# Respreading casts, evacuations and relus over ScalarE and VectorE, with smaller weight staging and deeper pools, in a fused window-attention and channel-mix kernel

## The chip, the cores and the metric

The kernel runs on one core of a Trainium2 chip. The metric is the device time of one execution in microseconds (us), as the median of several runs. TensorE is called PE here, VectorE DVE, ScalarE ACT and GpSimd POOL; SP is SyncE, whose queue issues nearly all transfers.

## The reference

Two stages follow each other. First comes attention over a sliding window of 128 positions plus 4 sink positions; then a channel mix works on the attention's output.

```python
# q, k, v: (4, 8, 768, 64) f32; n_sink = 4, window = 128
scores = (q @ k.T) / sqrt(64), kept where pos < 4 or 0 <= i - j < 128
a = softmax(scores);  x = a @ v, as (4, 768, 512)
# channel mix; w_k: (512, 1024), w_v: (1024, 512), w_r: (512, 512)
xk = mu_k * x + (1 - mu_k) * x_prev      # x_prev: x one position earlier
xr = mu_r * x + (1 - mu_r) * x_prev
k = relu(xk @ w_k);  v = (k * k) @ w_v;  r = sigmoid(xr @ w_r)
return r * v                             # (4, 768, 512) f32
```

## The kernel before

The work is cut into 12 units of 256 positions: batch b has tiles T = 0, 1, 2, and unit u = 3 b + T. The stages of a unit and the tiles that they fill are these.

- **prepare**: q, k and v (f32) land in `qs`, `ks`, `vs`, three buffers each. Half tiles of q and k are cast to bf16 into `qb` and `kb` (lines 526 and 529), transposed by PE into a PSUM bank (L550) and evacuated into `qt` and `kt` (L560). For k from unit 4 on and q from unit 8 on, a DMA transposes instead (L537, issued by SP). v is cast into `vb` (L575), which has a column of ones for the softmax sums. In the first unit of a batch POOL copies the sink keys (`ksink`), and PE and DVE make the sink values (`vsink`).
- **attend**: sink scores (L611) with an exponential into `es`; scores of two head pairs at a time (L635) into `sc`; ACT's exponential into `e` (L657); DVE's mask (L671); the product with `vb` (L682, L694); DVE's reciprocal (L707) and scaling into `x` (L710).
- **mix**: PE transposes `x` (L733), the result is evacuated into `xt` (L744), and DVE makes the difference `td` (L758) and eight pieces of `xk` and `xr` (L768).
- **ffn**: eight blocks of keys with `wk_sb` (L818), relu into `rl` (L827), DVE's square into `kk` (L831), two gates with `wr_sb` (L841), tanh into `th` (L847), four blocks of products with `wv_h` (L859), DVE's final product into `ob` (L868), and a store. The last unit's last product is cut in two (L788, L798).

The f32 weights are loaded in five transfers of 1 MB: `wka`, `wkb` (column halves of w_k), `wr`, `wva`, `wvb` (row halves of w_v). Each of the three matrices has f32 staging of its own, and DVE casts them in ten pieces to bf16 (L501, L503).

PSUM holds two double-bank tiles `sc` and four single banks (`bank`), which the transposes, keys, gates, values and products share.

No scheduler runs at execution time. A list `ORDER` gives for each of PE, DVE, ACT, POOL and SP the numbers of its operations in order, and every engine runs its list strictly in that order. The class `Plan` walks the lists with assumed costs to decide two things: which buffer of a pool each operation takes, and where PE's list gets filler matmuls (L879) on a tile `warm`, which keep PE's clock up while there is no work. Which engine does an operation is fixed in the source: for unit 0 DVE casts q, k and v and evacuates q; all other casts of q and k and all other evacuations are ACT's; POOL casts v from unit 1 on, and DVE casts all weights.

Of the kernel before, what the change touches and what calls it, by code (L numbers as in the profile page):

```python
# [17 lines left out]
CAST = {"k": "ACT", "q": "ACT"}  # L18

CAST0 = {"k": "DVE", "q": "DVE"}  # L20
EVAC0 = {"k": "ACT", "q": "DVE", "x": "ACT"}
# [14 lines left out]
LOADS = ("kq0", "v0", "kq1", "wka", "v1", "wkb", "wr", "wva", "wvb")  # L36
WCAST = ("DVE",) * 10
VCAST = ("DVE", "POOL")
# [6 lines left out]
        92, 89, 98, 105, 95, 116, 108, 113, 128, 141, 124, 119, 131, 137, 103, 148, 134, 157,  # L45
        155, 168, 219, 211, 207, 212, 220, 208, 160, 176, 165, 171, 183, 189, 215, 193, 200,
        223, 180, 216, 225, 237, 298, 186, 290, 302, 291, 303, 299, 294, 248, 295, 227, 235,
        231, 263, 232, 228, 260, 306, 266, 318, 240, 256, 245, 251, 310, 276, 269, 311, 283,
        326, 329, 308, 321, 314, 343, 315, 370, 378, 352, 366, 371, 379, 332, 367, 374, 382,
        337, 375, 384, 359, 348, 386, 396, 387, 421, 390, 274, 444, 391, 452, 445, 453, 426,  # L50
        407, 448, 456, 394, 449, 457, 460, 399, 464, 404, 465, 415, 462, 410, 430, 472, 499,
        578, 437, 468, 474, 504, 469, 525, 583, 526, 537, 485, 538, 533, 509, 529, 534, 530,
        477, 553, 482, 488, 493, 545, 511, 564, 518, 549, 541, 546, 543, 550, 601, 609, 605,
        602, 556, 610, 606, 567, 631, 613, 561, 572, 614, 617, 587, 619, 621, 594, 629, 622,
        634, 625, 639, 626, 642, 677, 689, 678, 681, 663, 690, 682, 645, 707, 685, 650, 686,
        695, 701, 670, 718, 705, 702, 693, 697, 710, 698, 760, 715, 761, 756, 768, 757, 769,
        721, 726, 764, 742, 765, 772, 749, 740, 784, 780, 774, 781, 795, 834, 830, 835, 842,
        831, 787, 843, 838, 792, 798, 860, 776, 803, 816, 839, 777, 823, 846, 848, 854, 858,
        855, 871, 910, 918, 906, 911, 907, 850, 863, 851, 919, 868, 936, 874, 914, 879, 915,
        930, 892, 924, 899, 931, 926, 947, 934, 922, 944, 939, 927, 976, 972, 977, 984, 973,  # L60
        985, 950, 980, 955, 958, 981, 988, 990, 965, 992, 996, 993, 997, 1012, 1000, 1013, 1004,
        1001, 1005, 1008, 1016, 1009, 1020, 1018, 1021, 1028, 1024, 1029, 1025,
    ),
    "DVE": (
        70, 91, 88, 93, 97, 71, 94, 99, 100, 107, 112, 101, 123, 109, 114, 110, 118, 115, 120,
        125, 143, 121, 126, 146, 144, 78, 145, 150, 79, 151, 152, 81, 164, 154, 104, 159, 147,
        175, 170, 161, 80, 162, 177, 166, 178, 167, 172, 153, 173, 82, 83, 202, 195, 196, 210,
        69, 197, 203, 204, 198, 206, 84, 85, 205, 199, 214, 218, 239, 293, 301, 222, 86, 305,
        87, 255, 297, 250, 233, 244, 229, 241, 242, 257, 246, 247, 252, 258, 253, 325, 320, 278,
        312, 279, 285, 280, 287, 322, 286, 327, 323, 328, 331, 316, 281, 289, 288, 282, 354,  # L70
        333, 334, 336, 369, 373, 338, 355, 339, 377, 361, 381, 362, 356, 363, 388, 275, 357,
        392, 364, 365, 398, 358, 403, 447, 451, 414, 455, 400, 459, 401, 409, 405, 406, 466,
        416, 417, 411, 412, 432, 433, 434, 439, 441, 440, 435, 470, 442, 481, 476, 528, 436,
        510, 487, 492, 478, 532, 479, 483, 443, 489, 484, 494, 490, 495, 540, 555, 560, 513,
        536, 514, 520, 516, 515, 522, 521, 547, 551, 523, 571, 517, 566, 557, 558, 604, 524,
        568, 569, 562, 563, 573, 574, 608, 633, 612, 616, 589, 592, 590, 638, 623, 635, 591,
        596, 598, 597, 627, 636, 640, 641, 593, 599, 644, 600, 665, 649, 646, 680, 692, 647,
        684, 651, 652, 714, 666, 688, 709, 672, 667, 674, 703, 668, 675, 673, 711, 725, 699,
        712, 676, 716, 720, 669, 717, 722, 723, 727, 759, 728, 763, 744, 767, 745, 751, 771,
        746, 753, 752, 741, 786, 782, 747, 755, 791, 797, 788, 789, 833, 793, 799, 802, 794,  # L80
        800, 748, 804, 845, 805, 754, 837, 778, 841, 825, 818, 821, 819, 820, 826, 829, 827,
        867, 856, 862, 822, 878, 909, 864, 873, 865, 852, 913, 869, 870, 875, 876, 880, 828,
        881, 917, 921, 894, 943, 897, 932, 895, 938, 896, 901, 905, 902, 945, 903, 940, 941,
        928, 949, 946, 954, 904, 951, 952, 898, 956, 975, 957, 960, 979, 961, 963, 987, 962,
        983, 967, 969, 970, 968, 971, 994, 964, 998, 1003, 1007, 1015, 1011, 1022, 1030, 1026,
    ),
    "ACT": (
        67, 68, 90, 111, 106, 96, 122, 117, 127, 130, 136, 142, 129, 132, 133, 149, 138, 163,
        135, 158, 156, 169, 174, 221, 213, 182, 209, 188, 184, 190, 201, 194, 179, 185, 224,
        181, 217, 226, 238, 187, 243, 292, 262, 300, 304, 296, 254, 249, 236, 264, 259, 265,  # L90
        261, 307, 267, 319, 268, 324, 277, 270, 284, 342, 340, 309, 330, 335, 344, 345, 347,
        353, 372, 380, 368, 420, 425, 383, 376, 360, 498, 418, 349, 385, 397, 422, 503, 423,
        402, 496, 454, 427, 446, 413, 450, 395, 458, 408, 461, 501, 577, 582, 575, 463, 431,
        473, 500, 438, 579, 475, 480, 505, 584, 527, 486, 491, 535, 531, 539, 559, 554, 512,
        519, 565, 580, 542, 544, 653, 570, 655, 603, 611, 607, 657, 632, 615, 618, 588, 659,
        637, 630, 620, 731, 595, 735, 643, 648, 679, 664, 691, 683, 729, 713, 708, 687, 671,
        696, 733, 808, 724, 706, 694, 719, 806, 762, 810, 758, 770, 743, 766, 812, 750, 785,
        790, 775, 773, 801, 882, 796, 836, 832, 844, 866, 861, 840, 817, 824, 849, 847, 884,
        859, 888, 886, 872, 877, 912, 908, 942, 920, 916, 893, 937, 925, 900, 935, 948, 923,
        953, 978, 974, 986, 959, 989, 982, 991, 966, 1014, 1002, 1006, 1010, 1019, 1017,  # L100
    ),
    "POOL": (
        77, 72, 73, 75, 76, 74, 102, 139, 140, 191, 192, 271, 273, 272, 350, 351, 428, 506, 429,
        585, 507, 661, 508, 586, 662, 737, 738, 739, 814, 815, 890, 891,
    ),
    "SP": (
        1, 3, 0, 2, 4, 5, 6, 7, 8, 11, 9, 10, 16, 12, 15, 13, 20, 14, 19, 17, 18, 21, 22, 25,
        23, 234, 24, 30, 341, 28, 35, 346, 313, 29, 317, 26, 33, 27, 389, 38, 34, 40, 31, 419,
        424, 36, 393, 497, 230, 32, 502, 37, 41, 43, 576, 39, 467, 44, 45, 581, 46, 47, 656, 42,
        548, 51, 654, 471, 52, 660, 658, 49, 552, 628, 57, 50, 48, 55, 56, 53, 730, 732, 736,  # L110
        58, 734, 54, 704, 61, 807, 811, 809, 813, 63, 700, 783, 64, 624, 62, 883, 59, 60, 885,
        889, 887, 857, 65, 853, 779, 66, 929, 933, 999, 995, 1023, 1031, 1027,
# [4 lines left out]
class Plan:  # L117
# [17 lines left out]
    def op(self, engine, cost, emit, rank, reads=(), writes=(), take=(), hold=(), port=False,  # L135
           lag=None, service=0.0, descs=128, mode=0):
        self.ops.append(dict(engine=engine, cost=cost, emit=emit, rank=rank, reads=list(reads),
                             writes=list(writes), take=list(take), hold=list(hold), port=port,
                             lag=90.0 if lag is None else lag, service=service, descs=descs, mode=mode))

    def schedule(self):
# [42 lines left out]
        while any(lines.values()):  # L184
# [35 lines left out]
            if o["service"]:  # L220

                descs = o["descs"]
# [9 lines left out]
                flying.append((dma, descs))  # L232
# [39 lines left out]
def kernel(  # L272
# [36 lines left out]
    for name in ("ks", "qs", "vs"):  # L309
        pool(name, 3, [128, 2, H, D] if name == "vs" else [128, H, 2, D], FP32)  # L310
    pool("kb", 3, [128, 2, H, D], BF16)
    pool("qb", 3, [128, 2, H, D], BF16)
    pool("kt", 4, [128, NP, 2, 128], BF16)
    pool("qt", 3, [128, NP, 2, 128], BF16)
# [5 lines left out]
    pool("xk", 3, [128, NC, 256], BF16)  # L320
    pool("xr", 3, [128, NC, 256], BF16)
    pool("kk", 2, [128, NF, 256], BF16)
    pool("rl", 4, [128, 2, 256], BF16)
    pool("th", 4, [128, Dm], FP32)
    pool("ob", 3, [128, Dm], FP32)
    pool("vb", 3, [128, 2, H, D + 1], BF16)
    buf = P.buf

    def tile1(shape, dtype, name):
        return const.tile(shape, dtype, name=name)  # L330


    def dve(n, rate=1.04):
        return 64.0 + rate * n

    def act(n):
        return 67.0 + 0.833 * n
# [593 lines left out]
```

## Time and profile before

| what | value |
|---|---|
| median of 5 runs (lowest to highest) | 172.39 us (172.27 to 172.66) |
| the profiled execution's own time | 172.39 us |
| its span, first to last instruction | 170.7 us |
| PE busy, matmuls | 163.0 us, 1624 |
| DVE busy, instructions | 148.5 us, 372 |
| ACT busy, instructions | 132.4 us, 219 |
| POOL busy, instructions | 26.9 us, 47 |
| DMA packets, bytes | 82803, 33.82 MB |
| filler matmuls (L879) | 44, 13.1 us |
| granted PE clock | 1.00 throughout |

The profiled execution's time equals the median of the runs; 1.7 us of it lie outside the span. Durations in the profile are those of single instructions. On DVE and ACT one instruction starts before the one ahead of it has ended, so the spacing of starts in a dense stretch is shorter than a duration. Matmuls overlap still more: a row's mean is a latency, and the spacing says what a matmul costs.

### The profile page before, as it was taken

The numbers are of one execution on the slowest core, as the hardware profiler recorded it, in microseconds if no ns is written. First come the engines' busy times: TensorE is split into PE (matmuls) and PEld (weight loads), VectorE is DVE, ScalarE is ACT, GpSimd is POOL, SyncE is SP. The second block draws the span as 40 slices with busy tenths as digits, with TensorE's granted clock in tenths as the row PEclk, the third lists the DMA queues.
The fourth block names the chain that finished last, engine by engine and source line by source line (L and its number), as shares of the span: only waits on it lengthen the run. The fifth ranks groups of instructions, "written<-read, shape, count | busy, mean of one in ns | idle before, by whom it ended". The sixth has DMA issues, their size and how long they took to land.

```text
span 170.7 us, 4235 instructions
## 1 busy us (share of the span) xinstructions
PE 163.0 (96%) x1624; PEld 107.9 (63%) x1624; DVE 148.5 (87%) x372; ACT 132.4 (78%) x219; POOL 26.9 (16%) x47
## 2 busy tenths in 40 slices
PE   7898988999999999999999999999999999999992
PEld 2345576575758567667658568577585775684751
DVE  2497998999899778899999999998999999999632
ACT  3169987999999999999879979977887938654330
POOL 6130080005400020124301200120300203000000
PEclk9999999999999999999999999999999999999999
DMA  4999999998968999999757998976989985030203
GB/s 103 234 272 376 287 284 359 352 257 188 297 171 212 224 254 254 162 231 208 187 131 142 256 226 222 227 147 175 174 232 180 185 205 139 0 127 0 108 15 123
DMA packets 82803, 33.82 MB, mean 198 GB/s; under 512 B 64736, under 2 KB 77280, under 8 KB 82784
## 3 DMA queue, kind: packets, MB, share of 16 engines
q1 hardware_dynamic: 81728, 33.56, 84.6%
q8 instruction: 12, 0.20, 0.5%
q10 hardware_dynamic: 1056, 0.00, 0.3%
q14 instruction: 7, 0.06, 0.1%
HBM read 24.12 MB, written 6.29 MB: 178 GB/s over the span
## 4 chain that ended last, share of the span: by engine, by line
PE 81%; DMA 6%; SPq 6%; POOL 2%; ACT 1%; DVE 1%; issue 1%
PE bank L818 24%; PE bank L859 24%; PE bank L841 12%; DMA vs<-in_v_dram 6%; PE sc L635 6%; PE bank L694 6%; PE bank L733 3%; SPq L377 3%; SPq L360 2%; PE bank L550 2%; PE bank L682 2%; PE bank L611 2%; POOL vb L575 2%; SPq L397 1%; PE bank L788 1%
## 5 line engine op out<-in xcount | busy, mean ns | idle before, releaser
L818 PE MATMUL bank<-xk,wk_sb 128*128 128x256 bf16 x384 | 48.9, 273 | 0.0
L657 ACT ACTIVATE e<-sc 128x1024 bf16<-128x1024 f32 (+1 forms) x48 | 45.0, 976 | 4.9 <-PE sc L635 4.9
L859 PE MATMUL bank<-wv_h,kk 128*128 128x512 bf16 x184 | 46.4, 379 | 0.0
L818 PEld LDWEIGHTS <-wk_sb 128*128 128x128 bf16 x384 | 35.6, 98 | 7.1 <-issue 0.2
L575 POOL CAST vb<-vs 128x512 bf16<-128x512 f32 x22 | 20.0, 918 | 109.8 <-DMA vs<-in_v_dram 83.0
L827 ACT ACTIVATE rl<-bank 128x512 bf16<-128x512 f32 x48 | 27.6, 609 | 9.1 <-PE bank L818 8.5
L671 DVE TENSOR_TENSOR e<-e,mask 128x1024 bf16<-128x1024 bf16 (+1 forms) x48 | 30.7, 649 | 0.4 <-ACT e L657 0.4
L859 PEld LDWEIGHTS <-kk 128*128 128x128 bf16 x184 | 16.7, 98 | 14.7 <-DVE kk L831 0.3
L841 PE MATMUL bank<-wr_sb,xr 128*128 128x512 bf16 x96 | 24.5, 379 | 0.2 <-DVE wr_sb L503 0.2
L831 DVE TENSOR_TENSOR kk<-rl 128x512 bf16<-128x512 bf16 x48 | 20.9, 448 | 4.2 <-ACT rl L827 4.0
L768 DVE SCALAR_TENSOR_TENSOR xr<-td,mu,xt 128x256 bf16<-128x256 bf16 x48 | 22.9, 492 | 0.1
L768 DVE SCALAR_TENSOR_TENSOR xk<-td,mu,xt 128x256 bf16<-128x256 bf16 x48 | 21.9, 483 | 0.2
L710 DVE TENSOR_TENSOR x<-bank,rec 128x256 bf16<-128x256 f32 x48 | 19.5, 417 | 0.6
L694 PE MATMUL bank<-vb,e 128*128 128x65 bf16 x352 | 18.8, 193 | 0.9 <-POOL vb L575 0.9
L694 PEld LDWEIGHTS <-e 128*128 128x128 bf16 x352 | 16.7, 97 | 3.1 <-issue 1.0
L847 ACT ACTIVATE th<-bank 128x512 f32<-128x512 f32 x24 | 14.1, 602 | 5.0 <-PE bank L841 4.8
L868 DVE SCALAR_TENSOR_TENSOR ob<-th,bank 128x512 f32<-128x512 f32 x23 | 15.7, 681 | 2.2 <-ACT th L847 1.7
L744 ACT COPY xt<-bank 128x512 bf16<-128x512 bf16 x24 | 14.1, 591 | 4.2 <-PE bank L733 3.8
L879 PE MATMUL bank<-warm 128*128 128x512 bf16 x44 | 13.1, 435 | 1.3 <-DVE warm L894 1.3
L841 PEld LDWEIGHTS <-xr 128*128 128x128 bf16 x96 | 9.0, 98 | 8.2 <-issue 0.4
L635 PE MATMUL sc<-qt,kt 64*128 64x128 bf16 (+1 forms) x256 | 14.0, 238 | 0.0
L635 PEld LDWEIGHTS <-kt 64*128 64x128 bf16 x256 | 8.9, 94 | 6.0 <-issue 3.6
(54 smaller groups left out, 159.4 us busy)
## 6 DMA issues: line engine op xcount, KB each, us to landing
vs<-in_v_dram SPq DMA_DIRECT2D x24, 256.0 KB, 5.0
out_dram<-ob SPq DMA_DIRECT2D x23, 256.0 KB, 3.4
ks<-in_k_dram SPq DMA_DIRECT2D x18, 256.0 KB, 5.1
qs<-in_q_dram SPq DMA_DIRECT2D x7, 512.0 KB, 6.2
qs<-in_q_dram SPq DMA_DIRECT2D x10, 256.0 KB, 4.1
wk<-in_moe_w_k_dram SPq DMA_DIRECT2D x2, 1024.0 KB, 8.6
wv<-in_moe_w_v_dram SPq DMA_DIRECT2D x2, 1024.0 KB, 12.3
ks<-in_k_dram SPq DMA_DIRECT2D x3, 512.0 KB, 7.6
```

The lines of the kernel that those rows point to most:

```text
L575: lambda g=g, copy=copy: copy(out=buf["vb", u][:, g, :, 0:D], in_=buf["v", u][:, g, :, :]), rank,
L635: nc.tensor.matmul(out=sc[:, a, o0:o1], lhsT=lhs[rows], rhs=rhs[rows], start=True, stop=True)
L657: nc.scalar.activation(out=buf[ek][:, :, lo:], in_=buf[sck][:, :, lo:], func=AF.Exp, scale=scale)
L671: nc.vector.tensor_tensor(out=at, in0=at, in1=m, op=ALU.mult)
L694: nc.tensor.matmul(out=o[:, g, a, :], lhsT=e[:, a, e0:e0 + 128], rhs=rhs, start=(T == 0 and i == 0), stop=(i == len(blocks) - 1), skip_gro ...
L710: P.op("DVE", dve(256), lambda ok=ok, rk=rk, c=c: nc.vector.tensor_tensor(out=buf["x", u][:, :, 128 * c:128 * c + 128].rearrange("p g (a d ...
L768: nc.vector.scalar_tensor_tensor(out=buf[key][:, c0 + i, :], in0=buf[tk][:, i, :], scalar=mu[w][:, c0 + i:c0 + i + 1], in1=xt[:, c0 + i, t ...
L818: nc.tensor.matmul(out=ps[:, i, :], lhsT=wk_sb[:, c, 128 * f:128 * f + 128], rhs=xk[:, c, :], start=(c == 0), stop=(c == NC - 1), skip_gro ...
L827: P.op("ACT", act(512), lambda psk=psk, rk=rk: nc.scalar.activation(out=buf[rk], in_=buf[psk].rearrange("p (i t) -> p i t", i=2), func=AF. ...
L831: P.op("DVE", dve(512, 0.52), lambda f2=f2, rk=rk: nc.vector.tensor_tensor(out=buf["kk", u][:, 2 * f2:2 * f2 + 2, :], in0=buf[rk], in1=buf ...
L841: nc.tensor.matmul(out=buf[psk], lhsT=buf["xr", u][:, c, 128 * g:128 * g + 128], rhs=wr_sb[:, c, :], start=(c == 0), stop=(c == NC - 1))
L859: nc.tensor.matmul(out=buf[psk], rhs=wv_h[:, f, :], lhsT=buf["kk", u][:, f, 128 * g:128 * g + 128], start=(f == 0), stop=(f == NF - 1))
```

## The change

The arithmetic is the same. These parts change.

- **Engines.** An operation may now carry alternatives (`alts`), and a table `CHOICE` (operation number to engine) picks one. Beside what was fixed before, 9 evacuations into `xt`, 5 casts of k, 5 of q, 3 evacuations into `qt` and 3 relus move from ACT to DVE (the relu as a `tensor_scalar_max` with 0 from PSUM); 2 casts of unit 0 (one each of k and q) and 4 of the 10 weight casts move from DVE to ACT; of 22 casts of v on POOL, 9 move to ACT and 7 to DVE.
- **Order.** All five lists of `ORDER` are new. SP's list loads q of unit 2 ahead of the weights; both halves of w_k come ahead of v of unit 1; the first half of v of unit 2 comes ahead of w_r. Unit 2's values stand much earlier in PE's list.
- **Weight staging.** A pool `w32` of three buffers [128, 4, 512] f32 replaces the staging of its own that each matrix had. The fourth and fifth load wait until a buffer's casts are done.
- **Pools.** `qt` 3 to 4, `xk` 3 to 4, `kk` 2 to 3, `rl` 4 to 5, `vb` 3 to 4. `kk`'s buffer is taken by the first relu instead of the first square.
- **Assumed costs of the walk.** An issue by SP 480 instead of 980 (and 60 per head instead of 115), a transfer of v 1330 instead of 1320, a weight transfer 3150 instead of 3040. With the new lists they decide the buffers and the number of fillers, which in the built program is 37 instead of 44.

```diff
-CAST = {"k": "ACT", "q": "ACT"}
-CAST0 = {"k": "DVE", "q": "DVE"}
-EVAC0 = {"k": "ACT", "q": "DVE", "x": "ACT"}
+CHOICE = {
+    80: "ACT", 82: "ACT", 84: "ACT", 86: "ACT", 93: "DVE", 94: "DVE", 97: "DVE", 99: "DVE", 100:
...
+}
-LOADS = ("kq0", "v0", "kq1", "wka", "v1", "wkb", "wr", "wva", "wvb")
-WCAST = ("DVE",) * 10
-VCAST = ("DVE", "POOL")
+LOADS = ("kq0", "v0", "kq1", "wka", "wkb", "v1", "wr", "wva", "wvb")
...
+        i = len(self.ops)
+        if i in CHOICE:
+            engine = CHOICE[i]
+            cost, emit, port = alts[engine]
...
+    pool("w32", 3, [128, NC, 512], FP32)
-    pool("qt", 3, [128, NP, 2, 128], BF16)
+    pool("qt", 4, [128, NP, 2, 128], BF16)
-    pool("xk", 3, [128, NC, 256], BF16)
+    pool("xk", 4, [128, NC, 256], BF16)
-    pool("kk", 2, [128, NF, 256], BF16)
-    pool("rl", 4, [128, 2, 256], BF16)
+    pool("kk", 3, [128, NF, 256], BF16)
+    pool("rl", 5, [128, 2, 256], BF16)
-    pool("vb", 3, [128, 2, H, D + 1], BF16)
+    pool("vb", 4, [128, 2, H, D + 1], BF16)
...
-        P.op("SP", 1000.0, lambda: nc.sync.dma_start(out=dst, in_=src), rank, service=service,
-             descs=512, writes=keys)
+        key = ("w32", name, i)
+        P.op("SP", 1000.0, lambda: nc.sync.dma_start(out=buf[key], in_=src), rank,
+             service=3150.0, descs=512, take=[("w32", key)], writes=[(name + "32", i)])
...
+                P.op("ACT", act(512), evacuate(nc.scalar.copy), r,
+                     alts={"ACT": (act(512), evacuate(nc.scalar.copy), False),
+                           "DVE": (dve(512, 0.54), evacuate(nc.vector.tensor_copy), True)},
+                     hold=[psk], reads=[psk],
...
+            def relu_dve(psk=psk, rk=rk):
+                nc.vector.tensor_scalar_max(
+                    out=buf[rk], in0=buf[psk].rearrange("p (i t) -> p i t", i=2), scalar1=0.0)
```

## The prediction

> **What bounds it now.** I read the busy time by stage first. Columns: stretch and length, then busy us and instruction count of PE, PEld, DVE, ACT, POOL, granted clock, DMA share, GB/s.
>
> ```profile
> 0.00:30.00 30.00, 25.84 (x239) 14.82 (x240) 22.15 (x62) 19.85 (x31) 8.86 (x21) 1.00 1.00 274
> 30.00:42.00 12.00, 11.71 (x104) 7.52 (x103) 11.76 (x28) 12.00 (x21) 1.57 (x2) 1.00 0.97 267
> 42.00:80.00 38.00, 38.00 (x411) 26.43 (x409) 33.97 (x83) 37.11 (x64) 6.81 (x10) 1.00 1.14 226
> 80.00:160.00 80.00, 80.00 (x825) 54.25 (x824) 77.37 (x195) 60.05 (x100) 9.65 (x15) 1.00 0.73 160
> 160.00:170.70 10.70, 7.46 (x53) 4.91 (x51) 3.22 (x8) 3.37 (x6) 0.00 (x0) 1.00 0.26 98
> ```
>
> From 42 to 160 us PE never rests. ACT is full from 30 to 80, DVE nearly so from 80 to 160. The chain of waits, in order of time, gives what matmuls cost in a dense stretch:
>
> ```profile
> 34.04 2.62 PE bank L818 x24
> 36.66 0.55 PE sc L635 x12
> ...
> 37.75 0.86 PE bank L859 x4
> 38.62 0.44 PE bank L611 x4
> 39.05 0.86 PE bank L859 x4
> 39.92 0.22 PE bank L550 x4
> ```
>
> Four key matmuls are 0.436 us (2.62/6), four products or gates 0.864, four transposes 0.22, a pair of scores 0.54 (0.40 for T = 0), sink scores 0.44; the same chain gives 0.37 for a values block (0.17 for T = 0). All of PE's useful work is then 96x0.436 (keys) + 46x0.864 + 4x0.436 (products) + 24x0.864 (gates) + 11.8 (scores) + 14.6 (values) + 10.7 (transposes) + 4.4 (sinks) = 145.6 us. The last matmul ends at 167.5, so PE loses 21.9 us. Call "loss" at a moment the time minus the useful work done: from the starts in the timeline it is 8.1 at the first scores (8.82), 11.1 at the first values (12.81), 16.4 at the first keys (21.89), 19.5 at the first products (37.59), 20.0 about 72 us and 21.9 at the end. The time is made in the first 38 us; the rest is packed. PE's timeline shows the loss as fillers:
>
> ```profile
> 9.25 1.47 PE L879 MATMUL bank<-warm 128*128 128x512 bf16 x6
> 13.24 1.24 PE L879 MATMUL bank<-warm 128*128 128x512 bf16 x5
> 19.33 1.94 PE L879 MATMUL bank<-warm 128*128 128x512 bf16 x8
> ```
>
> DVE's timeline gives its spacing, which is shorter than the durations:
>
> ```profile
> 17.27 0.48 DVE L768 SCALAR_TENSOR_TENSOR xr<-td,mu,xt 128x256 bf16<-128x256 bf16 x1
> 17.66 0.48 DVE L768 SCALAR_TENSOR_TENSOR xk<-td,mu,xt 128x256 bf16<-128x256 bf16 x1
> 18.06 0.69 DVE L503 CAST wk_sb<-wk 128x1024 bf16<-128x1024 f32 x1
> 18.66 0.48 DVE L768 SCALAR_TENSOR_TENSOR xk<-td,mu,xt 128x256 bf16<-128x256 bf16 x1
> ```
>
> A mix piece lasts 0.48 and costs 0.40; a weight cast lasts 0.69 and costs 0.60. Read like this, DVE's whole queue is 139.4 us dense, ACT's 124.8. POOL's longest wait:
>
> ```profile
> POOL vb L575 <- DMA vs<-in_v_dram: 83.0, 13, 14.7
> ```
>
> POOL waits 83 us for transfers of v, harmlessly, as nothing is queued behind them.
>
> **Parts: the loads.** The queue serves transfers in order; the trace's completions are 1.75 us apart for 512 KB of q or k, 1.2 for a half of v, 2.8 for a weight (one took 4.3). q of unit 2 now goes ahead of the weights, so these land 1.6 later: first half of w_k at 18.3 (16.6 before), second at 21.1, v of unit 1 at 24.5 (23.0). After that I add up: k2 26.3, v2 27.5 and 31.6 (before 40.4 and 41.2), wr 30.4, wva 34.4 to 35.9, wvb 37.2 to 38.6. Staging costs nothing here: wva's buffer is free after the first two casts (21.4 below), wvb's after ACT's cast of w_k (25.7), both before their turn at SP.
>
> **The start, queue by queue, with those spacings.** DVE's memsets for sinks, edges and ones (8.4 to 10.4 us before) now stand ahead of its first cast, in its idle time. Values of unit 0 start at 11.7 (12.81). Keys start when DVE has cast w_k: 20.5 (21.89). After six key blocks and unit 2's sink scores, values of unit 1 wait for v's casts on DVE: 25.2. Unit 1's keys start at 30.35 (33.2 before) with 12.75 us of useful work done: loss 17.6, against 19.4. Then ACT sets the pace: from 29.8 to 39.6 it does four relus and three tanhs (0.49 each), four exponentials and three weight casts (0.91 each, by the 1024-wide exponential), 9.8 us without a gap. The first product starts at 37.75 as before, but two values blocks (0.74), a gate (0.86) and sink scores (0.44) more are done. Loss 17.6 against 19.5: **the lead is 1.9 us**. A transfer late by more than 0.3 to 1 us (wva, wvb, k3) would eat into it.
>
> **The engines.** DVE: casts of k and q, net 8 x 0.335 = 2.7; v 7 x 0.335 = 2.3; `qt` 3 x 0.615 (its own two such rows) = 1.8; relus 3 x 0.60 (the f32 PSUM row of L868) = 1.8; weights -4 x 0.60 = -2.4. `xt` from PSUM in bf16 has no row: between 0.34 (`td`, same size from SBUF) and 0.615 (`qt`, strided, from PSUM), 9 pieces, 3.0 to 5.5; I take the lower end, as its rows are contiguous like `td`'s. Sum 9.2 to 11.7: 148.6 to 151.1. POOL's casts stretch DVE's instructions that run beside them (squares 0.39 to 0.83, median 0.42); summed over medians this is 4.1 us, and dropping 16 of 22 gives back 0 to 3. ACT: -9x0.48 - 8x0.515 - 3x0.58 - 3x0.49 + 9x0.515 + 4x0.91 = -3.4; the relief is early, the casts of v come after 80 us, where it has 20 us idle.
>
> What is late next is DVE. Adding DVE's queue from the first final product on (41.0 in my walk), it delivers what PE wants at 50, 52, 62 and 71.5 us, at loss 17.7, between 0.0 and 0.2 us too late, or 0.3 to 0.5 with the dearer `xt`. The same sum before left 0.9 at 46 and 57, 5 at 72. After 80 the cushion grows to 7. So PE gives back 0.2 to 0.5 for the sum and, with handovers and small waits, I say 0.5 in all. ACT at 37.1 of 38 us did the same before and PE lost only 0.3 there, which is why I don't take more. Deeper pools cost nothing and let PE run ahead. PE's tail is the same 5 us of gates and products after the last keys, the relus on DVE wait no longer than on ACT (0.60 against 0.49).
>
> Sum: -1.9 + 0.5 = -1.4, on the profiled execution's 172.39 (170.7 span and 1.7 outside), which equals the median: **171.0**.
>
> The Trainium skill's "ScalarE: Activation LUTs", "Rules for kernel authors", says relu belongs on VectorE, up to about three times faster per element. The row here speaks against it for an f32 PSUM source: 0.60 spacing on DVE (L868) against 0.49 on ACT (L827). By the rule three relus would add 0.5 us to DVE instead of 1.8, and the forecast would hardly move. "VectorE: DVE Perf Modes", in its cycle table and tier table, lets a 16-bit copy from PSUM run at double rate; from its (120 + 256) cycles at 0.96 GHz I estimate 0.39 us for `xt`, 3.5 us for nine.
>
> **Rivals.** (A) The whole lead is kept, since PE's useful work, not DVE, is still the bound: 170.5. For it: the ACT example. Against: DVE's sum has no cushion.
>
> (B) Slower: DVE becomes the bound between 42 and 80. Before, DVE fell 4.8 us behind its own dense sum between 42.8 and 69.8, though mostly as it waited for PE. If it falls behind by x, PE's loss at 71.5 is 17.7 + 0.2 + x against 20.0; from x = 2.1 on the change is slower. At 3.5, midway to the old lag, it is 1.4 slower: 173.8. Against: a queue with a backlog finds its inputs ready.
>
> (C) A late transfer: casts of v now stand in DVE's and ACT's strict queues, with masks and exponentials behind them, and PE behind those. A wait that POOL bore for nothing costs its length. One weight transfer took 1.5 longer than its twin; that much, once, makes 172.5, no difference. Twice makes it slower.
>
> (D) It does nothing: the lead is lost to the order of PE's list, 172.4.
>
> **Chances.** Forecast and the faster part around it 0.40, A 0.20, B 0.18, C 0.14 (half slower, a third no difference), D 0.08. Within 0.2% (0.35 us) is about what a measurement here cannot tell from no change. Faster 0.62, same 0.13, slower 0.25. The range runs from 169.7 (A, and under half of the 1.9 us that PE still loses after 72 us saved by the deeper pools) to 173.6 (B nearly at its price).
>
> **What would show it.** Right: first values near 11.7, keys near 20.5, PE's loss near 17.6 at the first product, DVE over 95% busy from 42 to 80 us, 127 to 130 us of ACT, under 15 of POOL; `xt` on DVE near 0.42 in duration. Wrong: v of unit 1 later than 25; gaps of PE between 42 and 80 of more than 2 us put down to DVE (B) or ACT or DVE waiting for `vs` (C); products that start late because w_v lands after 39.

## The result, and the profile after

| | before | after |
|---|---|---|
| median of the runs shown together (lowest to highest, runs) | 172.38 us (171.78 to 173.92, 50) | 172.92 us (171.92 to 173.64, 29) |
| ratio after to before, 95% interval | | 1.0028 (1.0015 to 1.0040) |
| the profiled execution's own time, span | 172.39, 170.7 us | 173.44, 171.7 us |
| PE, DVE, ACT, POOL busy | 163.0, 148.5, 132.4, 26.9 us | 162.6, 153.5, 129.6, 11.6 us |
| fillers | 44 | 37 |

The change makes the kernel slower, by 0.5 us, where 1.4 us less was forecast. On the chip of the experiments the unaltered changed kernel stood at 1.0009 (0.9993 to 1.0025), which cannot be told from no change; so by the medians it costs 0.5 us at most, and what needs an explanation above all is the 1.4 us that did not come. Its runs spread more than those of the kernel before (the middle half spans 0.7 us, against 0.3), and one profiled execution can lie 0.7 us to either side of its kernel's median; so several profiles are compared below.

The busy time by stage, columns as in the prediction:

```profile
0.00:30.00 30.00, 25.94 (x256) 15.70 (x256) 24.26 (x69) 22.96 (x36) 4.56 (x19) 0.94 1.01 264
30.00:42.00 12.00, 12.00 (x117) 7.83 (x112) 11.97 (x31) 11.58 (x18) 0.00 (x0) 1.00 1.06 320
42.00:80.00 38.00, 37.95 (x426) 26.57 (x424) 37.54 (x99) 35.60 (x60) 4.14 (x7) 1.00 0.94 214
80.00:160.00 80.00, 78.58 (x778) 52.81 (x777) 73.95 (x191) 57.63 (x96) 2.90 (x5) 1.00 0.74 158
```

ACT is relieved and DVE is full (37.54 of 38) between 42 and 80 us, as forecast. POOL's wait for v has shrunk with its casts:

```profile
POOL vb L586 <- DMA vs<-in_v_dram: 65.2, 3, 36.0
```

But PE, which never rested between 80 and 160 us before, now rests 1.4 us there. The chain of waits says on what. At the start (28 to 34 us):

```profile
28.68 0.06 issue
28.74 0.75 ACT kt L572
29.54 0.62 PE sc L650 x12
30.15 0.54 PE bank L904 x2
30.69 3.49 PE bank L835 x32
```

and later, around 87 and 110 us:

```profile
86.99 5.59 DMA vs<-in_v_dram
92.58 0.02 issue
92.60 0.02 ACT vb L586
...
109.98 5.48 DMA qt<-qb
115.46 0.04 issue
115.50 0.51 PE sc L650 x8
```

The first piece is the second half of v of unit 7, whose cast now stands in ACT's strict list. The second is a transposing transfer of q of unit 9. In the kernel before the same transfer lands at 115.9 us and the scores that need it start at 118.9; in after it lands at 115.5, and PE is ready for it 1.1 us earlier. So here the new lists brought the scores forward, and not the transfer back. For unit 11 it is the transfer that comes later: the last one, of k, lands at 142.2 us instead of 138.2, and the unit's scores start at 142.0 instead of 139.2. The waits from 80 to 160 us put their lengths beside them:

```profile
PE sc L650 <- DMA qt<-qb: 1.1, 1, 1.1
...
ACT vb L586 <- DMA vs<-in_v_dram: 1.2, 2, 0.7
```

"Loss" as in the prediction (time minus useful PE work, here at the first operation after the moment), from the timelines of the profiled executions; the last columns are the time from the last matmul to the end of the span, and the execution's own time:

| profile | 38 us | 60 | 80 | 100 | 120 | 160 | end | time |
|---|---|---|---|---|---|---|---|---|
| before | 19.52 | 19.91 | 20.22 | 20.83 | 21.14 | 21.68 | 3.22 | 172.39 |
| after | 17.91 | 18.75 | 19.15 | 20.35 | 21.85 | 22.36 | 3.59 | 173.44 |
| e0, after again | 18.17 | 19.11 | 19.88 | 20.49 | 21.50 | 22.00 | 3.51 | 173.03 |
| e1 | 18.06 | 18.92 | 19.33 | 19.91 | 20.27 | 21.21 | 3.57 | 172.26 |
| e3 | 18.13 | 18.86 | 19.26 | 19.91 | 20.27 | 20.89 | 3.53 | 171.89 |
| e14, e3 again | 18.49 | 19.41 | 19.81 | 20.46 | 20.83 | 21.61 | 3.61 | 172.71 |
| e12 | 18.16 | 19.10 | 19.50 | 19.84 | 20.20 | 20.58 | 3.57 | 171.66 |

From "before" to "after": -1.61 at 38 us, +0.54 up to 80 (1.24 lost against 0.70), +1.75 from 80 to 160 (3.21 against 1.46), +0.37 behind the last matmul. The sum is +1.05, which is 173.44 - 172.39. In this profile the lead was there, and it was lost after 80 us.

### The profile page after: what moved, and what is told of

It is laid out like the page before. It is cut to its first block, busy times and chain, and to the rows that moved or that the text cites. A ratio compares the mean times of both kernels' runs of the same rounds, so it can differ in the third digit from the quotient of the medians.

```text
span 171.7 us, 4214 instructions
## 1 busy us (share of the span) xinstructions
PE 162.6 (95%) x1617; PEld 107.7 (63%) x1617; DVE 153.5 (89%) x399; ACT 129.6 (75%) x209; POOL 11.6 (7%) x31
## 4 chain that ended last, share of the span: by engine, by line
PE 68%; DMA 9%; ACT 9%; DVE 8%; issue 2%; SPq 2%; DVEq 0%
PE bank L884 20%; PE bank L835 20%; PE bank L866 9%; PE sc L650 5%; PE bank L709 5%; DMA vs<-in_v_dram 3%; DMA qt<-qb 3%; ACT e L672 3%; DMA ks<-in_k_dram 3%; PE bank L748 3%; PE bank L564 2%; DVE e L686 2%; PE bank L697 2%; PE bank L626 1%; ACT rl L845 1%
## 5 line engine op out<-in xcount | busy, mean ns | idle before, releaser
L835 PE MATMUL bank<-xk,wk_sb 128*128 128x256 bf16 x384 | 49.6, 273 | 0.3 <-DVE wk_sb L508 0.3
L845 ACT ACTIVATE rl<-bank 128x512 bf16<-128x512 f32 x45 | 26.2, 607 | 15.4 <-PE bank L835 12.8
L866 PE MATMUL bank<-wr_sb,xr 128*128 128x512 bf16 x96 | 24.0, 379 | 0.0
L785 DVE SCALAR_TENSOR_TENSOR xr<-td,mu,xt 128x256 bf16<-128x256 bf16 x48 | 22.3, 482 | 0.0
L857 DVE TENSOR_TENSOR kk<-rl 128x512 bf16<-128x512 bf16 x48 | 19.4, 422 | 1.2 <-ACT rl L845 1.2
L586 POOL CAST vb<-vs 128x512 bf16<-128x512 f32 x6 | 4.9, 808 | 130.7 <-DMA vs<-in_v_dram 65.2
L697 PE MATMUL bank<-vsink,es 128*128 128x130 bf16 x64 | 12.5, 220 | 0.3 <-ACT rl L845 0.3
L904 PE MATMUL bank<-warm 128*128 128x512 bf16 x37 | 11.0, 430 | 1.3 <-DVE warm L919 1.3
```

Source lines behind the costliest of these rows:

```text
L697: nc.tensor.matmul(out=o[:, g, :, :], lhsT=buf["es", u][:, 128 * g:128 * g + 128], rhs=vsink[b % 2][:, 2 * c:2 * c + 2, :], start=True, st ...
L785: nc.vector.scalar_tensor_tensor(out=buf[key][:, c0 + i, :], in0=buf[tk][:, i, :], scalar=mu[w][:, c0 + i:c0 + i + 1], in1=xt[:, c0 + i, t ...
L835: nc.tensor.matmul(out=ps[:, i, :], lhsT=wk_sb[:, c, 128 * f:128 * f + 128], rhs=xk[:, c, :], start=(c == 0), stop=(c == NC - 1), skip_gro ...
L845: nc.scalar.activation(out=buf[rk], in_=buf[psk].rearrange("p (i t) -> p i t", i=2), func=AF.Relu)
L857: P.op("DVE", dve(512, 0.52), lambda f2=f2, rk=rk: nc.vector.tensor_tensor(out=buf["kk", u][:, 2 * f2:2 * f2 + 2, :], in0=buf[rk], in1=buf ...
L866: nc.tensor.matmul(out=buf[psk], lhsT=buf["xr", u][:, c, 128 * g:128 * g + 128], rhs=wr_sb[:, c, :], start=(c == 0), stop=(c == NC - 1))
```

## Experiments

Three theories were open. T1: transfers that come late after 80 us take the lead. T2: VectorE, full from 42 us on, is the bound. T3: the lead is only work that the other engines still owe. Each run stands beside runs of the kernel before on its chip; the ratio is to those. Lists in the cuts of the edits are shortened (`...`).

**e0, the changed kernel again.** 

> The changed kernel once more, unaltered. Both theories: about 172.9 us, 0.5 slower than before. T1 (two transfers that arrive late, the second half of v of unit 7 and the transpose of q of unit 9, take the lead between 95 and 116 us): the new profile shows the same two stalls of PE again, about 0.5 us near 96 and 1.2 us before the scores of unit 9 near 115.5, and a loss (time minus useful PE work) that goes from about 19.1 at 80 us to about 21.6 at 116. T2 (VectorE, 98.8% busy from 42 us on, is the bound): the stalls stand in other places and are put down to VectorE.

Measured: 172.62 us, 1.0009 (0.9993 to 1.0025). The loss goes from 19.88 at 80 us to 21.33 at 115.8. The stall at the scores of unit 9 is there again, 0.71 us by the loss and 0.6 by the waits, where it has the same name; the one near 96 us is not.

```profile
PE sc L650 <- DMA qt<-qb: 0.6, 1, 0.6
```

**e1, e2, e3: two moves in SP's list.** Operation 736 transposes q of unit 9, 57 loads half of q of unit 10, 41 and 42 load v of unit 7.

```diff
# e1                                     # e2 (e3: both)
- 730, 734, 57, 736, 54,                 - 37, 38, 41, 389, ... 471, 46, 42, 656,
+ 730, 734, 736, 57, 54,                 + 37, 38, 41, 42, 389, ... 471, 46, 656,
```

> SP issues the second transpose of q of unit 9 ahead of the first half load of q of unit 10 instead of behind it. T1: the transpose lands near 112 instead of 115.5, the 1.2 us stall of PE before the scores of unit 9 goes, and 0.8 to 1.2 us of it stays won: 171.7 to 172.1 us, at or below before. T2: PE's stall moves to a wait for VectorE within 20 us and the time stays within 0.2 us of 172.9.

> SP issues the second half of v of unit 7 right behind the first, 12 us earlier (near 76 instead of 87). T1: the cast of it on ScalarE waits no more, PE's stall near 96 goes and 0.3 to 0.5 us is won: 172.4 to 172.6 us; the loads of k and q behind it land 1.2 us later, which has cover of some us. T2: no change, 172.9 within 0.2.

> Both moves in SP's queue together. T1: they add, 1.1 to 1.7 us less than the changed kernel: 171.2 to 171.8 us, faster than before by 0.6 to 1.2. The loss at 116 us is then near 20, and near 21 at the end. T2: not below 172.5, as VectorE then is the bound.

Measured: e1 172.33 us, 0.9995 (0.9980 to 1.0010); e2 172.60, 1.0004 (0.9992 to 1.0016); e3 172.54, 1.0004 (0.9987 to 1.0022). In e1's profile the transpose lands at 111.3 instead of 115.5, the stall is gone, and the loss at 120 us is 20.27 instead of 21.50 to 21.85. Of that, 0.3 us arrives in the median (172.33 against e0's 172.62), and the intervals of the two overlap. e2 takes ACT's wait for v away and wins nothing in the median. e3 profiles 0.5 us below before (171.89 against 172.39), but its median does not follow. In e1 the next transposing transfer, of k of unit 11, ends a wait of PE's weight loads:

```profile
PEld L650 <- DMA kt<-kb: 0.6, 1, 0.6
```

**e4, e5, e6, e9: splices.** For each engine the list of one kernel up to a moment, then that of the other. The buffer of `kk` is taken by whichever relu of the unit comes first. The edit is given here as a rule; in the runs the lists are written out.

```diff
-ORDER[e] = after[e]
+ORDER[e] = [i in after[e] started before t] + [i in before[e] not yet in it]
# e4: t = 42; e9: t = 45.5; e6: t = 80; e5: before[e] first, after[e] behind, t = 42
```

> A splice: every engine follows the changed kernel's list and choice of engines up to the operations that it starts before 42 us, and from there on the list and the engines of the kernel before (pools, weight staging and code are the changed kernel's). T1 (the lead of 1.4 us at 42 us is real, and the changed kernel's later lists lose it): the loss is 18.0 at 42 us and grows by the 2.2 that the kernel before lost after it, so 171.0 us, up to 171.5 with what the seam costs. T3 (the lead is only work that VectorE and ScalarE still owe, and any list gives it back): 172.2 to 172.6 us.

> The opposite splice: lists and engines of the kernel before up to 42 us, of the changed kernel from there on. T1: loss 19.5 at 42 us, growing by the 3.8 to 4.4 that the changed kernel loses after it: 173.8 to 174.6 us. T3: 172.4 to 172.9 us, as the start makes no difference.

> The first splice with its seam at 80 us. T1 with the loss of the lead after 80 us (transfers that come late between 90 and 120 us): the loss at 80 us is 19.2 to 19.9 and grows by the 1.4 of the kernel before: 171.3 to 172.0 us. T1 with the loss between 42 and 80: 172 to 172.4. T3: 172.2 to 172.6.

> The splice of e4 with its seam at 45.5 instead of 42 us: by then units 2 and 3 have their k and q prepared and no operation of PE is out of the order of before's list. T1 (the lead is real, the later lists lose it): loss 18.0 to 18.2 at 45 us, growing by the 2.0 that both e4 and the kernel before lost after 50 us: 170.7 to 171.3 us. T3 (the lead is owed work, or transfers that arrive no earlier, and any list gives it back): loss back at 20 or more by 60 us, 172.2 us or more.

Measured: e4 173.67 us, 1.0072 (1.0054 to 1.0089); e5 175.85, 1.0203 (1.0177 to 1.0229); e6 172.96, 1.0017 (0.9993 to 1.0041); e9 175.48, 1.0156 (1.0119 to 1.0193). e4 and e9 do not test what they were built for, because the seam costs more than the lead: between 38 and 50 us e4's loss goes from 18.37 to 20.39, and e9 loses 2.48 us in one stall before unit 3's values at 48.5. Behind the seam they do show one thing. From 60 to 160 us before's lists lose 1.77 (before), 1.72 (e4) and 2.18 (e9), and 2.15 in e8 below; the changed lists lose 3.61, 2.89 (e0) and 2.76 (e5). e5 stands 2.1 us later than before at 60 us and still stalls 0.90 us at the scores of unit 9. So the changed lists run into these transfers without a lead, too. With e3's two moves they lose 2.03 us, and 2.20 in e14 below, about what before's lists do.

e6 shows the other side, and meets none of its expectations. By its loss it is 0.9 us ahead of the kernel before at 80 us; from there to 160 us it follows before's lists, on which PE never rested, and PE waits 1.4 us in three places (PE's waits of e6, 80 to 160 us):

```profile
PE bank L885 <- DVE kk L858: 0.5, 1, 0.5
PE bank L710 <- POOL vb L587: 0.5, 1, 0.5
PE sc L651 <- DMA kt<-kb: 0.4, 1, 0.4
```

The first is the seam (82.6 us); the others are a cast of v (137.7) and a transposing transfer of k at unit 9's scores (118.7). So a PE that is ahead meets late work on before's lists as well, and T3 cannot be put aside for this part.

**e7, casts of v back on GpSimd.**

```diff
-    428: "ACT", 506: "ACT", 507: "ACT", 586: "ACT", 661: "ACT", 662: "ACT",
-    737: "ACT", 738: "ACT", 815: "DVE", 890: "ACT",
# and ORDER: these ten from ACT's and DVE's lists into POOL's, as v lands; with e3's moves
```

> Both moves in SP's queue as in e3_both, and ten casts of v from unit 5 on go back to GpSimd (nine from ScalarE, one from VectorE), in the order in which v lands. If casts that wait for v in ScalarE's and VectorE's strict queues cost the lead (the prediction's case C), 0.3 to 0.6 us less than e3_both: 171.9 to 172.2 us, and a narrower spread of its runs, as only GpSimd waits for v. If not: 172.5 within 0.2, or up to 0.5 more where GpSimd's casts stretch VectorE's instructions.

Measured: 173.80 us, 1.0072 (1.0048 to 1.0096). It is 1.3 us slower than e3, not faster. DVE's mix pieces last 503 ns instead of 491 in the groups, and PE loses 0.56 us before the product with `spread` at 70.6, where it waits for a cast on POOL. These two do not account for all of the 1.3 us, whose rest stays open. With e2, where a wait of ACT for v goes and nothing is won, this speaks against the prediction's case C in the form it was given.

**e8, pools and staging alone.** `ORDER` and the engines are those of before, in the changed code.

> The changed kernel's code (deeper pools, weight staging in three halves, assumed costs) with all lists and engines of the kernel before. If the pools or the staging cost or give anything: a difference of over 0.3 us from before. All theories here put the difference into lists and engines: 172.4 us, within 0.3 of before, loss 21.7 at the end.

Measured: 172.51 us, 1.0005 (0.9994 to 1.0017). Pools, staging and assumed costs do nothing by themselves that these runs can tell.

**e10, e11.** e10 is e3 with the loads of unit 11 (61 to 64) and v of unit 10 (60) ahead of a store (779); e11 takes nine casts and evacuations after 90 us from DVE.

```diff
# e10, SP's list
-811, 779, 60, 63, 61, 62, 64, 783,
+811, 60, 63, 61, 62, 64, 779, 783,
# e11, CHOICE, and ORDER accordingly
-595: "DVE", 659: "DVE", 664: "DVE", 731: "DVE", 743: "DVE", 824: "DVE", 900: "DVE", 959: "DVE", 966: "DVE",
```

> e3_both, and the store of unit 7's product (which waits for its final product at 126 us) stands behind the loads of k and q of unit 11 in SP's queue instead of ahead of them and of v of unit 10. T1: these loads land 1 to 2 us earlier, the transposes of unit 11 too, PE no longer waits for the last of them near 141 us (0.2 to 0.6 us in the profiles) and the runs spread less: 172.0 to 172.3 us. Else 172.5 within 0.2.

> e10, and nine casts and evacuations from 90 us on (two casts of q, seven evacuations into xt) go back from VectorE to ScalarE: VectorE 3.0 us less, ScalarE 4.4 us more, where it was 25% idle. T2 (VectorE is the bound after 80 us): 0.5 to 1.0 us less than e10. T1: within 0.2 of e10, as PE waits for transfers and not for VectorE there.

Measured: e10 172.61 us, 1.0003 (0.9989 to 1.0017), no gain. In its profile the last transfer of k of unit 11 lands at 140.7 us, as in e3's, so the move did not bring it forward. e11 174.00, 1.0104 (1.0083 to 1.0125), 1.4 us slower than e10. With its work moved, DVE waits for ACT, whose strict list is now too long in the wrong places (waits of e11, 90 to 125 us):

```profile
DVE kk L857 <- ACT rl L845: 1.9, 1, 1.9
...
DVE td L775 <- ACT xt L757: 1.7, 2, 1.1
```

So e11 shows only that this relief does not help. What tells against T2 from 80 us on is e12, next, where DVE keeps its list and the time falls.

**e12, e13: cheaper transposing transfers.** The 24 transfers become plain copies of the same bytes, in the changed kernel (e12) and in the one before (e13).

```diff
-nc.sync.dma_start_transpose(out=buf[key][:, :, half, :], in_=buf[rk][:, half, :, :].rearrange("p h d -> p (h d)"))
+nc.sync.dma_start(out=buf[key][:, :, half, :], in_=buf[rk][:, half, :, :].rearrange("p (c a) d -> p c (a d)", a=2))
```

> The changed kernel, where the 24 transfers that transpose k (from unit 4) and q (from unit 8) are plain copies of the same size from kb or qb into kt or qt: the scores are then of untransposed data, and their times are those of the same instructions. Issue and landing of each are shorter. T1 (PE, 1.4 us ahead, has run into the transfers, and their spread goes into the time): 1.0 us or more less than the changed kernel, 171.2 to 171.9 us, and the runs within 1 us of each other. If transfers are not it (VectorE or ScalarE is): 172.4 to 172.9.

> The same replacement of the 24 transposing transfers by plain copies in the kernel before. T1: its lists leave these transfers 0.8 us and more, so nothing changes: 172.2 to 172.5 us. If such transfers were a bound in any list: 0.5 us less or more, as in the changed kernel.

Measured: e12 171.70 us (171.54 to 172.24, six runs), 0.9961 (0.9945 to 0.9976); e13 172.75 (172.05 to 173.16), 1.0017 (1.0004 to 1.0031). The same edit takes 0.9 to 1.2 us from the changed kernel and closes the spread of its runs; in the kernel before it takes nothing, and adds 0.3, whose cause was not sought. T1 holds: what holds the changed kernel back after 80 us is the transposing transfers. What is it that got cheaper? The issue rows of after, then of e12 (KB each where the row has it, median us from issue to landing):

```profile
kt<-kb SPq DMA_TRANSPOSE x16, 2.5
...
qt<-qb SPq DMA_TRANSPOSE x8, 3.2
```

```profile
kt<-kb SPq DMA_DIRECT2D x16, 128.0 KB, 2.4
qt<-qb SPq DMA_DIRECT2D x8, 128.0 KB, 2.8
```

In the median a copy lands hardly sooner. The one that PE waited for does: q of unit 9, issued right behind a load, takes 5.48 us to land in after (shown above) and 3.34 in e12 (issued at 108.84, landed at 112.18). With stores of a quarter of the bytes (e17 below) it still takes 4.72. The transfer engines are less busy too, a share of 0.66 from 80 to 160 us against 0.74 in after, at the same bytes (e12, columns as above):

```profile
80.00:160.00 80.00, 80.00 (x792) 53.95 (x791) 75.76 (x197) 57.95 (x97) 3.04 (x5) 1.00 0.66 157
```

SP's own timeline shows another difference, first after, then e12 (start, time that SP spends on the issue):

```profile
109.31 0.57 SPq L379 DMA_DIRECT2D qs<-in_q_dram  x1
109.98 1.22 SPq L551 DMA_TRANSPOSE qt<-qb  x1
111.25 0.57 SPq L369 DMA_DIRECT2D vs<-in_v_dram  x1
```

```profile
108.12 0.62 SPq L379 DMA_DIRECT2D qs<-in_q_dram  x1
108.84 0.60 SPq L551 DMA_DIRECT2D qt<-qb  x1
109.49 0.62 SPq L369 DMA_DIRECT2D vs<-in_v_dram  x1
```

A transposing issue holds SP for 1.2 us, a copy for 0.6. In the changed kernel 18 of them stand between 82 and 140 us, 22 us of SP's strict list, with the loads of the next units behind them. With half of that, and with less work for the transfer engines, the loads, the casts, and the transposes of units 9 and 11 all come earlier: in e12 the last transpose of each lands 1.7 and 2.0 us before the scores that need it, where in after and e0 both land only as these scores start. How much of the gain is SP's issue and how much the transfer behind it was not separated: no run changes one alone.

**e14, e3 again.** 

> e3_both once more, to see a second execution of it in the profile, since its first profiled one was 0.65 us under the median of its runs. If a typical run loses that time in stalls that differ from run to run: a profile near 172.5 us with one or two stalls of PE of 0.3 us or more behind transfers. If the profiled execution is 171.89 us again, the difference lies between profiled and other runs, and no trace shows it.

Measured: 172.73 us (171.48 to 173.27), 1.0000 (0.9978 to 1.0023), profiled at 172.71. Beside e3's profile it loses 0.36 more by 38 us, 0.19 from 38 to 60, and 0.16 from 120 to 160 us, 0.08 at the end; the largest stall that e3 did not have is 0.30 us (values of unit 2, 38.2 us). So this run, near the median, loses its 0.8 us in small pieces in several places, not in one stall that an edit could remove.

**e15, e16, e17.**

```diff
# e15 (on e3): 20 stores, in POOL's list by the time their products are ready
-nc.sync.dma_start(out=out[b, s0:s0 + 128, :], in_=buf[bk])
+nc.gpsimd.dma_start(out=out[b, s0:s0 + 128, :], in_=buf[bk])
# e16 (on e3): CHOICE, and ORDER accordingly
-272: "DVE",
# e17 (on the changed kernel)
-nc.sync.dma_start(out=out[b, s0:s0 + 128, :], in_=buf[bk])
+nc.sync.dma_start(out=out[b, s0:s0 + 128, 0:128], in_=buf[bk][:, 0:128])
```

> e3_both, and 20 of the 25 output stores are issued by GpSimd, which is 90% idle, instead of SP, in the order in which the products are ready, so that a load or a transposing transfer no longer stands behind a store that waits (26 us of SP's waits in the profile of e14). If SP's strict queue is what makes the transfers late (T1, by the queue): transfers land earlier, 0.5 to 1.0 us less than e3: 171.6 to 172.0 us, runs within 1 us of each other. If it is the service of the transfers themselves, or GpSimd's issuing disturbs VectorE: 172.5 us or more.

> e3_both, and the cast of the second half of v of unit 3 goes back from VectorE to GpSimd, where nothing is queued ahead of it: PE waits 0.4 us for it at 50.7 us in the profiles, behind some 3 us of VectorE's backlog (T2 in the small, the prediction's give-back). If that wait is VectorE's: the loss at 60 us falls by 0.2 to 0.4, and the time by as much at most, 172.1 to 172.5 us; if the next of VectorE's operations takes its place: no change, 172.5 within 0.2.

> The changed kernel, whose 23 whole stores write only the first 128 of 512 columns, so a quarter of the bytes (4.4 MB less of 33.8); the rest of the output is not written. Lists and all instructions are the same, transposing transfers included. If the load on the transfer engines in general is what makes the transposing transfers and v late: 0.5 to 1.0 us less than the changed kernel, 171.7 to 172.3. If it is these transposing transfers themselves (service and SP's issue of them), as in e12: 172.5 to 172.9.

Measured: e15 174.16 us, 1.0104 (1.0074 to 1.0134). It only moves the strict queue: POOL now waits for products with casts of v behind it (waits, 60 to 165 us), and nothing is learned of SP.

```profile
POOL out_dram L903 <- DVE ob L893: 78.6, 16, 16.9
```

e16: 172.40 us, 0.9994 (0.9980 to 1.0009). PE's wait at 50.9 stays, and 0.25 us at 51.8 come with it; the loss at 60 us does not fall (19.32). So the give-back near 50 us is not that cast alone, and may be DVE's backlog as a whole. e17: 172.39 us, 0.9994 (0.9970 to 1.0018); the stall at the scores of unit 9 is still there (0.44). Less traffic may help a little; its interval reaches into both expectations.

No version with the reference's output beats both kernels (e12 and e13 leave out the transposition, e17 most of the output): e1 and e16 are 0.2 to 0.6 us below the changed kernel's two medians and cannot be told from before.

## Why the prediction was wrong, step by step

**The start: right, a little short.** First keys at 20.3 us (20.5 forecast), values of unit 1 at 25.1 (25.2), keys of unit 1 at 30.5 (30.35), first product at 38.2 (37.75). The loss there is 17.9 to 18.5 in the profiles of the table instead of 17.6, so the lead is 1.0 to 1.6 us and not 1.9. Part of the shortfall is there at unit 1's keys, 17.8 to 18.1 us of loss instead of 17.6. A stall on the way to them is shown above: PE loses about 1 us waiting for the evacuation of unit 2's `kt` by ACT at 28.7, and 0.45 more behind the scores.

**Durations: right.** The copy into `xt` from bf16 PSUM lasts 419 ns on DVE (0.42 was said), and in a dense stretch the next instruction starts 0.33 us after it, the lower end that was taken; the prediction's estimate from "VectorE: DVE Perf Modes", 0.39, lies between the two. A relu lasts 676 ns on DVE and 607 on ACT. The Trainium skill's "ScalarE: Activation LUTs", "Rules for kernel authors", gives its threefold for bf16, which these rows with an f32 source do not test. The groups of after (count, busy us, mean ns, idle before):

```profile
L845 ACT ACTIVATE rl<-bank 128x512 bf16<-128x512 f32 x45 | 26.2, 607 | 15.4 <-PE bank L835 12.8 <-issue 1.1 <-DVE kk L857 1.1
...
L757 ACT COPY xt<-bank 128x512 bf16<-128x512 bf16 x15 | 8.8, 590 | 1.3 <-PE bank L748 1.1
...
L757 DVE COPY xt<-bank 128x512 bf16<-128x512 bf16 x9 | 3.8, 419 | 1.6 <-PE bank L748 1.6
...
L849 DVE TENSOR_SCALAR rl<-bank 128x512 bf16<-128x512 f32 x3 | 2.0, 676 | 0.8 <-PE bank L835 0.8
```

**The give-back from 42 to 80: about right.** 0.5 was said; 0.54 in after, 0.43 in e3, 0.64 in e12, 1.0 in e0 (each beyond the 0.70 that before loses). Rival B had no place: with DVE at 98.8% the cost is half a microsecond to one.

**After 80 us: this step failed.** "After 80 the cushion grows to 7. So PE gives back 0.2 to 0.5 for the sum" was a sum over DVE's list alone. DVE's cushion was indeed enough (e12 keeps DVE's list), but SP's list was walked only to the last weight at 38.6 us. Its 18 transposing transfers, 1.2 us of issue each, and its stores that wait stand after that, and the new lists bring the scores of units 9 and 11 up against them. The term set at 0 is 0.7 (e0) to 1.75 us (after). e12 shows what it is made of: with copies in their place, PE loses 1.08 from 80 to 160, less than before does, and the time is 171.70.

It is the largest term, not the only one. e0's profile lies 2.0 us above the forecast: 0.55 from the shorter lead, 0.5 from the give-back, 0.7 after 80 us, 0.3 at the end. In e14, where the stall at unit 9 is gone, a lead of 1.0 is still spent on 0.6 up to 80 us, 0.3 after it and 0.4 at the end. The prediction's signs of being right came true, but for the loss at the first product: first values at 11.0 to 11.3 us, keys at 20.3 to 20.6, 98.8% of DVE, 129.6 us of ACT, 11.6 of POOL. All of them are totals or lie before 80 us, so none could show this step failing.

**Case C** had the right kind of cause and the wrong place. The cast of v that PE waited for costs nothing in the median (e2), and moving casts of v back is worse (e7); the transfers that count are the transposing ones, behind loads and stores in SP's list. Its chance, 0.14, was too low for a change that reorders a list which nobody had walked.

**The end** was taken as unchanged. The span ends 3.5 to 3.6 us behind the last matmul in the changed kernels of the table (3.2 before), as the last two stores take 2.2 and 2.1 us instead of 1.7 and 1.8 to land. Why stays open.

With e12's numbers the forecast's sum reads -1.36 + 0.64 - 0.38 + 0.35 = -0.75 (171.66 - 172.39 = -0.73): this is about what the change is worth where transfers keep up. With copies in both kernels, e12 against e13, it is 1.05 in the medians, 0.3 of which is e13's unexplained loss.

## What to carry to other kernels

When lists of several strict queues are reordered, walk every queue to its end, and the one that issues transfers first: its own issue time per transfer is a cost like any other, and a wait in front of it is a wait for all that stands behind. A stall that a profile names and an edit removes is worth what the median says, not its length; where runs spread over more than the effect, compare medians of many runs, and several profiles. To tell a late transfer from a slow engine, make the transfer cheaper in both kernels: the one that is bound by it answers, the other does not.

## Not expected of the hardware

- An SBUF-to-SBUF transposing transfer of 128 KB costs SP 1.21 us of issue (median of 24, after) and lands 2.5 us after its issue began in the median, but 5.48 us right behind a load of q; a plain copy of the same size costs 0.60 (e12), and lands after 2.4 and 3.34 us in these places. So the issue doubles, and behind other transfers the landing is later too.
- The granted clock fell to about half for 3.4 us near 15 us in some executions of the changed kernel's start and not in others: the windows of 14 to 18 us show 0.59 in after, 0.63 in e0, and 1.00 in e12 and e3, with PE busy 2.86, 2.80, 2.86 and 2.80 of 4.00 us in the window before. It did not show in the loss (14.45 us at 21 us in after, 14.66 in e3). The Trainium skill's "TensorE: Matmul & The Clock Gate", in its part on the clock gate, has the clock halve after an idle window of about 3.4 us; the length agrees, but PE was 70% busy here, and equally busy windows ended either way; why stays open.
